# Retention and a multiplicative feed-forward on one core: the third chunk loaded and worked ahead of the weights

## The chip, the core and the metric

The kernel runs on one core of a Trainium2 chip. The metric is the device time of one execution in microseconds (us). The profile is of one execution, and its span runs from the first to the last instruction of the program. TensorE does the matrix products (PE in the profile, its weight loads PEld), VectorE is DVE, ScalarE ACT, GpSimd POOL, and SyncE SP; SP issues all transfers here.

## What is computed

```python
def _attn_ref(q, k, v):                      # (4, 8, 768, 64) each
    gamma = 1.0 - 2.0 ** (-5.0 - np.arange(H))
    for t in range(S):
        state = gamma[None, :, None, None] * state + np.einsum('bhd,bhe->bhde', k[:, :, t], v[:, :, t])
        y[:, :, t] = scale * np.einsum('bhd,bhde->bhe', q[:, :, t], state)

def _moe_ref(x, w1, w2, w3, w_out):          # x: y as (3072, 512)
    a = x @ w1                               # 512 x 1024
    b = x @ w2                               # 512 x 1024
    h = a * b @ w3                           # 1024 x 1024
    return h @ w_out                         # 1024 x 512
```

A recurrent retention over 768 steps for 4 batches and 8 heads gives x, 3072 tokens of 512 numbers. A feed-forward with a product of two branches follows. All inputs and the output are float32.

## The kernel before

The retention is done in chunks of 128 tokens, 24 in all (`NSTEP`, numbered n), six to a batch. Within a chunk, `scores(n)` (L353) multiplies keys by queries on TensorE, and VectorE masks the result (L364). `kv(n)` (L372) makes keys times values, adds the state carried so far (L390, VectorE) and decays it (L391, GpSimd, "t"). `outputs(n)` (L394) adds the two parts of y and scales them into a tile `XT` of two chunks (L407, VectorE). The inputs of a chunk are loaded by `load_chunk` (L67): q for two chunks at each even n (512 KB in pieces of 512 bytes), k and v for each (256 KB each in pieces of 256 bytes). `casts(n)` (L264) turns them into float16 on GpSimd: q at L270, k at L276, v times a decay at L280 ("vp"). Queries and keys are then transposed: in chunks 0 to 7 on TensorE (`q_transposes`, L288, `transposes`, L337), from chunk 8 on by transfers (`dma_transposes`, L317; "kT" and "qTd"). ScalarE copies the keys into a padded tile KP (L350 and L194 in the early chunks, L342 and L343 later), which the scores wait for.

w3 and w_out depend on no token, so their product is made once at the start (L215 to L258) and replaces both; the chunk's feed-forward is then (x w1)*(x w2) times that product. All weights come as float32 rows of 512 KB into twelve staging tiles (`wst`) and are cast to float16 by ScalarE (L194) or VectorE (L192) with `cast_to`.

The feed-forward goes by blocks of tokens (`bounds`, L517): 256, then 128 and 128, then 256 each. `a_unit` (L434) multiplies by w1 and has ScalarE copy the result to a tile `pa`; `b_unit` (L439) multiplies by w2, and VectorE takes the product of both into HT (L443); `o_unit` (L448) multiplies by the combined weights, and ScalarE scales into `osb`, which SP writes out. A unit is a short run of products: 0.43 us for a or b and 1.73 us for o in the kernel's own list of costs.

The order of the work is written out by hand until chunk 3 (L558 to L682). Each engine takes its instructions in the order written here, and SP issues its transfers in that order too. Block 0 is made row by row of the weights (`by_rows`, L617), so that each row can be used as soon as it is there: four PSUM banks (`four_banks`, L612) hold the eight products with w1, which are copied to two staging tiles (`hold`), and then those with w2. From chunk 4 on, `step(n)` (L519) puts units from a queue (`Queue`, L487) between the parts of the retention: 25% of its share after the scores, 25% after kv, the rest after the outputs. Units become available when their tokens are done.

PSUM has eight banks: one for the tag psT (transposes of keys), psA0, psA1, psK and psY with one each, and three in rotation for psF. In the four-bank products before the change, psF gives three and psY one.

The order of the loads is: four column blocks of w3 alternating with w_out, four rows of w3, chunks 0 and 1, four rows of w1, four of w2, chunks 2 to 5 (L115 to L125); chunks 6 and 7 are issued at L666 and L671.

Of the kernel before, what the change touches and what calls it, by code (L numbers as in the profile page):

```python
# [9 lines left out]
FP = mybir.dt.float32  # L10
HP = mybir.dt.float16
# [7 lines left out]
def kernel(  # L19
# [11 lines left out]
    nc = tc.nc  # L31
# [7 lines left out]
    NP = H // 2  # L39
# [27 lines left out]
    def load_chunk(n):  # L67
        if n >= NSTEP:
            return
        b, c = divmod(n, NCH)  # L70
        tiles = []
        if c % 2 == 0:

            t = ld.tile([128, 2 * 512], FP, tag="q64", name="q64", bufs=3)
            dma_in(
                t[:, :].rearrange("p (h x) -> p h x", x=2 * D),
                q[b, :, c * C : (c + 2) * C, :].rearrange("h (p t) d -> p h (t d)", t=2),
            )
            q_in[n // 2] = t
        for nm, src in (("k", k), ("v", v)):  # L80
            t = ld.tile([128, 512], FP, tag=nm + "32", name=nm + "32")
            dma_in(
                t[:, :].rearrange("p (h d) -> p h d", d=D),
                src[b, :, c * C : (c + 1) * C, :].rearrange("h i d -> i h d"),
            )
            tiles.append(t)
        chunk_in[n] = tiles

    def new_stage():
        return wstage.tile([128, 1024], FP, tag="wst", name="stg")  # L90
# [26 lines left out]
        w3c_st.append(load_w3_columns(i))  # L117
        wo_st.append(load_wo(i))
    w3_st = {f: load_rows(moe_w3, f) for f in range(4, 8)}
    load_chunk(0)  # L120
    load_chunk(1)
    w1_st = [load_rows(moe_w1, d) for d in range(4)]
    w2_st = [load_rows(moe_w2, d) for d in range(4)]
    for n in range(2, 6):
        load_chunk(n)  # L125


# [120 lines left out]
    def w3_mm(f, between=None):  # L248
        t = w3t.pop(f)
        ps = ps_f.tile([128, DM], FP, tag="psF", name="psW")  # L250
        for g in range(8):
            if g == 4 and between:
                between()
            nc.tensor.matmul(  # L254
                ps[:, :], lhsT=t[:, g * 128 : (g + 1) * 128], rhs=WO[g // 2][:, g % 2, :],
                start=(g == 0), stop=(g == 7),
            )
        cast_to(W3O[f][:, :], ps[:, :], False)  # L258
# [3 lines left out]
    Tst = [None]  # L262

    def casts(n):  # L264
        if n >= NSTEP:
            return
        k32, v32 = chunk_in.pop(n)
        if n % 2 == 0:
            q16 = att.tile([128, 1024], HP, tag="q16", name="q16")
            nc.gpsimd.tensor_copy(  # L270
                q16[:, :].rearrange("i (t h d) -> i h t d", t=2, d=D),
                q_in.pop(n // 2)[:, :].rearrange("i (h t d) -> i h t d", t=2, d=D),
            )
            q16s[n // 2] = q16
        k16 = att.tile([128, 512], HP, tag="k16", name="k16", bufs=3)
        nc.gpsimd.tensor_copy(k16[:, :], k32[:, :])  # L276
        vp = VP[n % 3]

        for r in range(2):
            nc.gpsimd.tensor_tensor(  # L280
                vp[:, :, r, r * 64 : r * 64 + 64],
                v32[:, :].rearrange("j (p s e) -> j p s e", s=2, e=64)[:, :, r, :],
                VS[:, :].rearrange("j (p s) -> j p s", s=2)[:, :, r].unsqueeze(2).broadcast_to((128, NP, 64)),
                MULT,
            )
        k16s[n] = k16

    def q_transposes(m, later=False):  # L288

        if m >= DT0 // 2:  # L290
            return
        q16 = q16s.pop(m)
        if m == 0:
            ps = ps_at.tile([128, NP, 2, 128], HP, tag="psA0", name="psTq")
        elif m == 1:
            ps = ps_at.tile([128, NP, 2, 128], HP, tag="psK", name="psTq")
        else:
            ps = ps_f.tile([128, NP, 2, 128], HP, tag="psF", name="psTq")
        for p in range(NP):
            for t in range(2):  # L300
                c0 = t * 512 + p * 128
                nc.tensor.transpose(ps[:, p, t, :], q16[:, c0 : c0 + 128], ident16[:, :])  # L302

        def back(c, on_dve=True):
            qT = att.tile([128, NP, 128], HP, tag="qT", name="qT", bufs=4)
            cast_to(
                qT[:, :, :].rearrange("p a (t i) -> p (a t) i", t=2),
                ps[:, :, :, c * 64 : (c + 1) * 64].rearrange("p a t i -> p (a t) i"), on_dve,
            )
            qTs[2 * m + c] = qT  # L310

        if later:
            return back
        back(0)
        back(1)
# [37 lines left out]
    def scores(n):  # L353
        kp = KP[n % 2]
        am = att.tile([128, NP, 2, 128], HP, tag="am", name="am")
        for half in range(2):
            ps = ps_at.tile([128, 2, 2, 128], FP, tag=f"psA{half}", name=f"psA{half}")
            for i in range(2):
                p = half * 2 + i
                for r in range(2):  # L360
                    nc.tensor.matmul(  # L361
                        ps[:, i, r, :], lhsT=kp[:, p, r, :], rhs=queries(n, p), start=True, stop=True
                    )
            nc.vector.tensor_tensor(  # L364
                am[:, half * 2 : half * 2 + 2, :, :].rearrange("j p s i -> j (p s) i"),
                ps[:, :, :, :].rearrange("j p s i -> j (p s) i"),
                keep[:, :].unsqueeze(1).broadcast_to((128, 4, 128)),
                MULT,
            )
        ATs[n] = am  # L370
# [44 lines left out]
    class Ffn:  # L415
# [17 lines left out]

        def a_unit(self, f):  # L434
            ps = self.mm(W1, f)
            self.pa[f] = fsb.tile([128, TB], FP, tag="pa", name="pa")
            nc.scalar.copy(self.pa[f][:, :], ps[:, :])  # L437

        def b_unit(self, f):  # L439
# [102 lines left out]
    def cast_w(W, st, d, on_dve):  # L542
        cast_to(W[d][:, :], st[d][:, :], on_dve)
# [38 lines left out]
    cast_w3(7, w3_st[7])  # L582
    casts(0)
    casts(1)
    w3_mm(5)
    w3_transpose(7)
    q_transposes(0)
# [4 lines left out]
    w3_mm(7, lambda: transposes(1))  # L592
    outputs(0)
    Tst[0] = t_new
    cast_w(W1, w1_st, 0, False)
    scores(1)
    outputs(1)
    Tst[0] = kv(1)
    cast_w(W1, w1_st, 1, False)
    cast_w(W1, w1_st, 2, False)  # L600
    cast_w(W1, w1_st, 3, True)
    cast_w(W2, w2_st, 0, True)
    cast_w(W2, w2_st, 1, True)


    ffn = [Ffn(a, b - a) for a, b in zip(bounds, bounds[1:])]
    NT = len(ffn)
    f0 = ffn[0]
    hold = [new_stage() for _ in range(2)]
    f0.HT = fsb.tile([128, 8, TB], HP, tag="ht", name="ht", bufs=3)  # L610

    def four_banks():  # L612
        got = [ps_f.tile([128, 2, TB], FP, tag="psF", name="psF") for _ in range(3)]
        last = ps_at.tile([128, NP, 128], FP, tag="psY", name="psYf")
        return [t[:, :, :] for t in got] + [last[:, :, :].rearrange("p (a b) c -> p a (b c)", a=2)]

    def by_rows(W, ps, d):  # L617
        for f in range(8):
            nc.tensor.matmul(  # L619
                ps[f // 2][:, f % 2, :], lhsT=W[d][:, f * 128 : (f + 1) * 128],  # L620
                rhs=XT[0][:, d, :], start=(d == 0 and f % 2 == 0),
                stop=(d == 3 and f % 2 == 1),
            )

    ps = four_banks()
    for d in range(4):
        by_rows(W1, ps, d)
    pa = [hold[i // 2][:, i % 2 * 512 : i % 2 * 512 + 512].rearrange("p (a n) -> p a n", a=2) for i in range(4)]
    for i in range(4):
        cast_to(pa[i], ps[i], i % 2 == 1)  # L630
    cast_w(W2, w2_st, 2, True)
    cast_w(W2, w2_st, 3, False)
    casts(2)
    ps = four_banks()
    for d in range(4):
        by_rows(W2, ps, d)
    for i in range(4):
        nc.vector.tensor_tensor(f0.HT[:, 2 * i : 2 * i + 2, :], pa[i], ps[i], MULT)  # L638
    q_back = []

    def chunk2_inputs():
        q_back.append(q_transposes(1, True))
        q_back[0](0)
        transposes(2)
        q_back[0](1, False)

    def chunk2_scores():
        scores(2)

    f0.o_unit(0, chunk2_inputs)  # L650
    f0.o_unit(1, chunk2_scores)
    casts(3)
    transposes(3)

    for t in range(1, NT):
        late = ffn[t - 1].o_units() if t > 1 else []
        units = ffn[t].ab_units()
        for i in range(0, len(units), 8):
            fill.units += units[i : i + 8] + late[:1]
            late = late[1:]  # L660
        fill.units += late
# [2 lines left out]


    load_chunk(6)  # L666
    t_new = kv(2)
    casts(4)
    outputs(2)
    Tst[0] = t_new  # L670
    load_chunk(7)  # L671
    scores(3)
    fill.run(2)
    t_new = kv(3)
    fill.run(2)
    casts(5)
    outputs(3)
    Tst[0] = t_new
    transposes(4)
    fill.run(1)  # L680
    q_transposes(2)
    fill.run(1)  # L682

    for n in range(4, NSTEP):
        if n != DT0 - 2:
# [33 lines left out]
```

## Time and profile before

| | us |
|---|---|
| median of 4 runs | 196.56 |
| lowest and highest | 196.12, 197.86 |
| the profiled execution: its time | 197.86 |
| the profiled execution: its span | 196.0 |
| its TensorE busy time | 185.2 |
| its VectorE, ScalarE, GpSimd busy time | 114.4, 97.2, 79.9 |

The profile's page shows busy time by engine, and in forty slices of 4.9 us each how full every engine was, in tenths. The chain of waits goes back from the last instruction to whatever released each one. Groups of instructions give the count, the busy time, the mean duration in ns and the idle time ahead of them, with what ended it. The busy time of TensorE includes time in which products overlap in its pipeline, so the pace is better read from start to start. A transfer's time to landing counts from its issue on SP, and includes all that it waits behind.

### The profile page before, as it was taken

To read this page: it belongs to the slowest core of one execution; us is meant where nothing else is said; L and a number is where in the kernel's file an instruction comes from. 1 tells how busy PE (TensorE), PEld (TensorE's weight loads), DVE (VectorE), ACT (ScalarE), POOL (GpSimd) and SP (SyncE) were. 2 spreads that over 40 slices of the span, in tenths; PEclk is the share of its full clock that TensorE was granted. 3 is DMA by queue.
4 is the path that set the end of the run, shared out by engine and by line. 5 is a ranking of instruction groups with operands and counts; after the bars stand their busy time and mean duration, and the time that the engine had idled before them with its cause. 6 is when DMAs were issued, how large, how long until landed. Compare 5 with 4: busy or idle time off the path is not lost.

```text
span 196.0 us, 4673 instructions
## 1 busy us (share of the span) xinstructions
PE 185.2 (95%) x1781; PEld 140.2 (72%) x1781; DVE 114.4 (58%) x215; ACT 97.2 (50%) x189; POOL 79.9 (41%) x137
## 2 busy tenths in 40 slices
PE   6589996999999999999999999999999999999993
PEld 2234565856998879679777887788778877887752
DVE  3224476955877767467565866585557655854220
ACT  6278648407454553546355644464455445533322
POOL 7300260347976756574523444844235442200000
PEclk9999999999999999999999999999999999999999
DMA  6999999979999999999999989979999731111003
GB/s 207 360 389 388 206 306 408 349 152 245 229 255 213 236 197 234 233 183 258 183 222 239 193 184 204 241 194 179 200 243 203 149 99 31 59 54 54 39 32 146
DMA packets 87590, 40.15 MB, mean 205 GB/s; under 512 B 67984, under 2 KB 82576, under 8 KB 87568
## 3 DMA queue, kind: packets, MB, share of 16 engines
q1 hardware_dynamic: 87568, 39.86, 90.0%
q8 instruction: 14, 0.23, 0.5%
q14 instruction: 8, 0.07, 0.1%
HBM read 29.36 MB, written 6.29 MB: 182 GB/s over the span
## 4 chain that ended last, share of the span: by engine, by line
PE 78%; DMA 10%; SPq 3%; DVE 3%; ACT 2%; issue 1%; POOL 0%; ACTq 0%; POOLq 0%; DVEq 0%
PE psF L427 35%; PE psO L453 19%; DMA stg<-in_moe_w_dram 5%; PE psA L361 5%; PE psW L254 4%; DMA v<-in_v_dram 3%; PE psF L619 2%; PE psY L399 2%; PE psY L400 2%; SPq L62 2%; PE psY L402 2%; DMA kT<-k 2%; PE psK L382 2%; SPq L326 1%; PE psTq L302 1%
## 5 line engine op out<-in xcount | busy, mean ns | idle before, releaser
L427 PE MATMUL psF<-xt,w 128*128 128x256 f16 (+1 forms) x768 | 87.1, 264 | 0.0
L427 PEld LDWEIGHTS <-w 128*128 128x128 f16 x768 | 68.0, 98 | 6.8
L443 DVE TENSOR_TENSOR ht<-pa,psF 128x256 f16<-128x256 f32 x88 | 36.7, 417 | 24.9 <-PE psF L427 10.6
L437 ACT COPY pa<-psF 128x256 f32<-128x256 f32 x88 | 32.7, 372 | 35.6 <-PE psF L427 35.1
L364 DVE TENSOR_TENSOR am<-psA,keep 128x512 f16<-128x512 f32 x48 | 30.9, 685 | 22.4 <-PE psA L361 22.4
L453 PE MATMUL psO<-w3o,ht 128*128 128x512 f16 x184 | 43.6, 379 | 0.2 <-DVE ht L638 0.2
L391 POOL TENSOR_TENSOR t<-s,GS 128x512 f16<-128x512 f32 x16 | 20.7, 1294 | 44.4 <-DVE s L390 37.7
L280 POOL TENSOR_TENSOR vp<-v,VS 128x256 f16<-128x256 f32 x48 | 28.6, 616 | 11.5 <-PE psY L402 5.3
L453 PEld LDWEIGHTS <-ht 128*128 128x128 f16 x184 | 17.7, 98 | 17.4 <-DVE ht L638 1.0
L458 ACT ACTIVATE osb<-psO 128x512 f32<-128x512 f32 x23 | 13.7, 597 | 31.5 <-PE psO L453 31.5
L270 POOL CAST q<-q 128x1024 f16<-128x1024 f32 x12 | 12.4, 1036 | 24.2 <-DMA q<-in_q_dram 24.2
L407 DVE TENSOR_TENSOR xt<-psY,YS 128x512 f16<-128x512 f32 x24 | 17.7, 736 | 4.6 <-PE psY L402 3.4
L276 POOL CAST k<-k 128x512 f16<-128x512 f32 x24 | 14.7, 613 | 8.6 <-PE psK L382 7.0
L399 PE MATMUL psY<-am,vp 128*128 128x128 f16 x96 | 16.7, 219 | 1.0 <-DVE am L364 0.9
L361 PEld LDWEIGHTS <-kp 128*128 128x128 f16 x192 | 12.5, 98 | 6.0 <-ACT kp L194 0.7
L400 PE MATMUL psY<-am,vp 128*128 128x128 f16 x96 | 16.7, 219 | 0.0
L212 DVE COPY w3t<-psW 128x1024 f16<-128x1024 f16 x8 | 5.5, 691 | 12.7 <-PE psW L220 9.5
L390 DVE TENSOR_TENSOR s<-psK,t 128x512 f32<-128x512 f32 x16 | 11.0, 689 | 3.1 <-PE psK L382 2.8
L342 ACT COPY kp<-kT 64x512 f16<-64x512 f16 x16 | 9.9, 618 | 4.1 <-DMA kT<-k 3.9
L194 ACT CAST w3h<-stg 128x1024 f16<-128x1024 f32 x8 | 8.3, 1043 | 5.0 <-DMA stg<-in_moe_w_dram 5.0
L400 PEld LDWEIGHTS <-vp 128*128 128x128 f16 x96 | 9.4, 98 | 1.5 <-issue 1.2
L361 PE MATMUL psA<-qTd,kp 128*128 128x128 f16 x128 | 9.9, 219 | 0.3 <-ACT kp L343 0.3
(69 smaller groups left out, 174.5 us busy)
## 6 DMA issues: line engine op xcount, KB each, us to landing
stg<-in_moe_w_dram SPq DMA_DIRECT2D x16, 512.0 KB, 8.7
q<-in_q_dram SPq DMA_DIRECT2D x12, 512.0 KB, 5.3
k<-in_k_dram SPq DMA_DIRECT2D x24, 256.0 KB, 5.4
v<-in_v_dram SPq DMA_DIRECT2D x24, 256.0 KB, 5.7
out_dram<-osb SPq DMA_DIRECT2D x23, 256.0 KB, 2.6
stg<-in_moe_w_out_dram SPq DMA_DIRECT2D x4, 512.0 KB, 8.9
kT<-k SPq DMA_TRANSPOSE x16, 4.3
out_dram<-osb SPq DMA_DIRECT2D x2, 128.0 KB, 1.7
```

Source lines behind the costliest of these rows:

```text
L276: nc.gpsimd.tensor_copy(k16[:, :], k32[:, :])
L280: nc.gpsimd.tensor_tensor(vp[:, :, r, r * 64 : r * 64 + 64], v32[:, :].rearrange("j (p s e) -> j p s e", s=2, e=64)[:, :, r, :], VS[:, :]. ...
L361: nc.tensor.matmul(ps[:, i, r, :], lhsT=kp[:, p, r, :], rhs=queries(n, p), start=True, stop=True)
L364: nc.vector.tensor_tensor(am[:, half * 2 : half * 2 + 2, :, :].rearrange("j p s i -> j (p s) i"), ps[:, :, :, :].rearrange("j p s i -> j ( ...
L391: nc.gpsimd.tensor_tensor(t16[:, :, :], s32[:, :, :], GS[:, :, :], MULT)
L399: nc.tensor.matmul(ps[:, p, :], lhsT=vp[:, p, 0, :], rhs=am[:, p, 0, :], start=True, stop=False)
L400: nc.tensor.matmul(ps[:, p, :], lhsT=vp[:, p, 1, :], rhs=am[:, p, 1, :], start=False, stop=(c == 0))
L407: nc.vector.tensor_tensor(XT[n // 2][:, :, n % 2 * C : (n % 2 + 1) * C].rearrange("p a (i t) -> p a t i", t=2), ps[:, :, :].rearrange(orde ...
L427: nc.tensor.matmul(ps[:, i * w : (i + 1) * w], lhsT=W[d][:, (f + i) * 128 : (f + i + 1) * 128], rhs=XT[self.tok0 // TB][:, d, c0 : c0 + w] ...
L437: nc.scalar.copy(self.pa[f][:, :], ps[:, :])
L443: nc.vector.tensor_tensor(self.HT[:, f : f + TB // self.width, :].rearrange("p f n -> p (f n)"), self.pa.pop(f)[:, :], ps[:, :], MULT,)
L453: nc.tensor.matmul(psO[:, :], lhsT=self.HT[:, f, tb * 128 : (tb + 1) * 128], rhs=W3O[f][:, :], start=(f == 0), stop=(f == 7),)
```

## The change

Chunk 2 is loaded ahead of w1 and w2, and is cast (`casts(2)`) right after chunk 1. Its query and key transposes, its scores, its `kv(2)` and its `outputs(2)` move ahead of or between the products of block 0 with w1. One row of w1 is cast on GpSimd instead of ScalarE. The w1 products of block 1 (chunk 2, 128 tokens: four a-units of two 128-column blocks each) are made between the w1 and the w2 products of block 0, and are held in a third staging tile. The bank psT takes the place of psY in the four-bank products. The last two rows of w2 are taken bank by bank, not row by row. The four b-units of block 1 follow, with chunk 3's key transposes between them. The o-units of block 0 are put at the head of the queue. Loads of chunk 7 and the casts and transposes of chunks 4 and 5 change places with other work.

```diff
-    load_chunk(0)
-    load_chunk(1)
+    for n in range(3):
+        load_chunk(n)
     w1_st = [load_rows(moe_w1, d) for d in range(4)]
     w2_st = [load_rows(moe_w2, d) for d in range(4)]
-    for n in range(2, 6):
+    for n in range(3, 6):
         load_chunk(n)
...
         def a_unit(self, f):
             ps = self.mm(W1, f)
-            self.pa[f] = fsb.tile([128, TB], FP, tag="pa", name="pa")
+            if f not in self.pa:
+                self.pa[f] = fsb.tile([128, TB], FP, tag="pa", name="pa")
             nc.scalar.copy(self.pa[f][:, :], ps[:, :])
...
     casts(1)
+    casts(2)
     w3_mm(5)
...
     outputs(0)
     Tst[0] = t_new
-    cast_w(W1, w1_st, 0, False)
     scores(1)
+    q_back = q_transposes(1, True)
+    q_back(0)
+    transposes(2)
     outputs(1)
+    q_back(1, False)
+    nc.gpsimd.tensor_copy(W1[0][:, :], w1_st[0][:, :])
     Tst[0] = kv(1)
     cast_w(W1, w1_st, 1, False)
+    scores(2)
     cast_w(W1, w1_st, 2, False)
-    cast_w(W1, w1_st, 3, True)
-    cast_w(W2, w2_st, 0, True)
-    cast_w(W2, w2_st, 1, True)
...
-    hold = [new_stage() for _ in range(2)]
+    hold = [new_stage() for _ in range(3)]
...
-        last = ps_at.tile([128, NP, 128], FP, tag="psY", name="psYf")
-        return [t[:, :, :] for t in got] + [last[:, :, :].rearrange("p (a b) c -> p a (b c)", a=2)]
-
-    def by_rows(W, ps, d):
-        for f in range(8):
+        got = [ps_t.tile([128, 2, TB], FP, tag="psT", name="psTf")] + got
+        return [t[:, :, :] for t in got]
+
+    def by_rows(W, ps, d, fs=range(8)):
+        for f in fs:
...
-    for d in range(4):
-        by_rows(W1, ps, d)
+    by_rows(W1, ps, 0)
+    t_new = kv(2)
+    by_rows(W1, ps, 1)
+    by_rows(W1, ps, 2)
+    cast_w(W1, w1_st, 3, True)
+    outputs(2)
+    Tst[0] = t_new
+    by_rows(W1, ps, 3)
...
-        cast_to(pa[i], ps[i], i % 2 == 1)
+        cast_to(pa[i], ps[i], i % 2 == 0)
+    cast_w(W2, w2_st, 0, True)
+
+    for f in range(0, 8, 2):
+        ffn[1].pa[f] = hold[2][:, f * 128 : f * 128 + 256]
+        ffn[1].a_unit(f)
+    cast_w(W2, w2_st, 1, True)
     cast_w(W2, w2_st, 2, True)
     cast_w(W2, w2_st, 3, False)
-    casts(2)
+    casts(3)
     ps = four_banks()
-    for d in range(4):
-        by_rows(W2, ps, d)
+    by_rows(W2, ps, 0)
+    by_rows(W2, ps, 1)
+    for i in range(4):
+        for d in range(2, 4):
+            by_rows(W2, ps, d, (2 * i, 2 * i + 1))
     for i in range(4):
         nc.vector.tensor_tensor(f0.HT[:, 2 * i : 2 * i + 2, :], pa[i], ps[i], MULT)
...
-    f0.o_unit(0, chunk2_inputs)
-    f0.o_unit(1, chunk2_scores)
-    casts(3)
+    ffn[1].b_unit(0)
+    ffn[1].b_unit(2)
     transposes(3)
-
-    for t in range(1, NT):
-        late = ffn[t - 1].o_units() if t > 1 else []
+    ffn[1].b_unit(4)
+    ffn[1].b_unit(6)
+
+    fill.units = f0.o_units()
+    for t in range(2, NT):
+        late = ffn[t - 1].o_units()
...
     load_chunk(6)
-    t_new = kv(2)
+    load_chunk(7)
+    fill.run(1)
+    scores(3)
     casts(4)
-    outputs(2)
-    Tst[0] = t_new
-    load_chunk(7)
-    scores(3)
-    fill.run(2)
     t_new = kv(3)
-    fill.run(2)
-    casts(5)
+    fill.run(1)
     outputs(3)
     Tst[0] = t_new
+    casts(5)
+    q_transposes(2)
     transposes(4)
-    fill.run(1)
-    q_transposes(2)
-    fill.run(1)
+    fill.run(2)
```

More of the change, by code (lines that the diff above doesn't have):

```diff
@@ L294, in q_transposes @@
             ps = ps_at.tile([128, NP, 2, 128], HP, tag="psA0", name="psTq")
-        elif m == 1:
-            ps = ps_at.tile([128, NP, 2, 128], HP, tag="psK", name="psTq")
         else:
@@ L625 @@
     ps = four_banks()
-    for d in range(4):
-        by_rows(W1, ps, d)
+    by_rows(W1, ps, 0)
[6 more added lines that the diff above has]
+    by_rows(W1, ps, 3)
     pa = [hold[i // 2][:, i % 2 * 512 : i % 2 * 512 + 512].rearrange("p (a n) -> p a n", a=2) for i in range(4)]
     for i in range(4):
-        cast_to(pa[i], ps[i], i % 2 == 1)
+        cast_to(pa[i], ps[i], i % 2 == 0)
[4 more added lines that the diff above has]
+    cast_w(W2, w2_st, 1, True)
     cast_w(W2, w2_st, 2, True)
     cast_w(W2, w2_st, 3, False)
-    casts(2)
+    casts(3)
     ps = four_banks()
-    for d in range(4):
-        by_rows(W2, ps, d)
+    by_rows(W2, ps, 0)
[3 more added lines that the diff above has]
+            by_rows(W2, ps, d, (2 * i, 2 * i + 1))
     for i in range(4):
         nc.vector.tensor_tensor(f0.HT[:, 2 * i : 2 * i + 2, :], pa[i], ps[i], MULT)
[L639 to L648, printed above, removed]
-    f0.o_unit(0, chunk2_inputs)
-    f0.o_unit(1, chunk2_scores)
-    casts(3)
-    transposes(3)
-    for t in range(1, NT):
-        late = ffn[t - 1].o_units() if t > 1 else []
+    ffn[1].b_unit(0)
+    ffn[1].b_unit(2)
+    transposes(3)
+    ffn[1].b_unit(4)
[3 more added lines that the diff above has]
+        late = ffn[t - 1].o_units()
         units = ffn[t].ab_units()
```

## The prediction, as made before the result was known

> **What bounds the kernel now.** I read the page's busy rows first, then the table of stretches, TensorE's waits, the chain of waits and, around its odd places, the timeline and the transfers' times to landing. The table of stretches gives, for each stretch, its length and the busy time of each engine; the last three numbers are the granted clock, the share of DMA time and GB/s.
>
> ```profile
> PE 185.2 (95%) x1781; PEld 140.2 (72%) x1781; DVE 114.4 (58%) x215; ACT 97.2 (50%) x189; POOL 79.9 (41%) x137
> PE   6589996999999999999999999999999999999993
> DMA  6999999979999999999999989979999731111003
> ```
> ```profile
> 24.00:37.40 13.40, 11.82 (x119) 8.73 (x118) 10.02 (x16) 6.91 (x11) 5.25 (x8) 1.00 1.02 360
> 37.40:41.30 3.90, 3.84 (x32) 3.02 (x31) 2.00 (x4) 1.54 (x3) 0.00 (x0) 1.00 1.03 207
> 41.30:53.30 12.00, 11.34 (x141) 8.43 (x141) 8.81 (x17) 5.87 (x12) 9.90 (x14) 1.00 1.02 222
> 53.30:81.40 28.10, 27.85 (x333) 23.53 (x332) 19.60 (x39) 13.01 (x29) 19.13 (x27) 1.00 1.20 225
> 81.40:196.00 114.60, 111.32 (x1043) 87.72 (x1043) 64.98 (x126) 54.85 (x119) 39.52 (x52) 1.00 0.80 157
> ```
> TensorE is the bound from about 24 us on, at full clock. The DMA engines are just as full until 81 us (shares of 1.02 to 1.20), and only after that do they have room. So there are two bounds in the stretch that the change rewrites. A moved product can gain only TensorE's idle time, and only if no transfer sets a later date that TensorE must keep anyway.
>
> TensorE's named waits after 30 us are few:
>
> ```profile
> PE psY L399 <- DVE am L364: 0.9, 1, 0.9
> PE psF L619 <- DVE xt L407: 0.6, 1, 0.6
> PE psA L361 <- ACT kp L194: 0.4, 1, 0.4
> PE psO L453 <- DVE ht L638: 0.2, 1, 0.2
> ```
> Taking each matmul at the pace of the chain (0.055 us for 128 moving columns, 0.109 for 256, 0.217 for 512) and counting from start to start, TensorE idles some 2.4 us in 24 to 37.4 us and 2.4 us in 37.4 to 53.3 us, of which 1.8 us lie between the end of the w2 products (41.2) and chunk 4's scores (53.33). That is the purse. The chain of waits names the second bound:
>
> ```profile
> 70.59 5.98 DMA v<-in_v_dram
> 76.58 3.62 DMA kT<-k
> 80.19 0.02 issue
> ...
> 80.86 0.62 ACT kp L343
> 81.48 0.05 issue
> 81.53 0.56 PE psA L361 x7
> ```
> The scores of chunk 9 wait for the transposed keys kT, which land at 80.2 us, and then for ScalarE's copies. TensorE idles 0.51 us there. Why is kT late? Its k16 was cast at 67.70 to 68.31, but its issue on SP comes at 76.58, behind the loads of chunks 10 and 11 and an output. From 20 to 98 us SP's issues follow each other within 0.1 us but for a few: SP is held back by the transfers in front, not by TensorE. GpSimd shows the same: its casts start as data lands.
>
> ```profile
> 63.97 1.04 POOL L270 CAST q<-q 128x1024 f16<-128x1024 f32 x1 [0.54 <-DMA q<-in_q_dram]
> ```
>
> **The change, part by part.**
>
> *Chunk 2 ahead of the weights.* Issue plus time to landing gives the dates: last v of chunk 1 22.65+4.6 = 27.2 us; first w1 row 23.69+5.5 = 29.2; last w2 row 28.26+10.0 = 38.3; chunk 2's q 29.17+12.3 = 41.5, k 42.5, v 43.65. The weight rows land about 1.3 us apart. Moved in front, chunk 2's three transfers push all eight rows. Cost from above: as they ran before, 43.65-38.27 = 5.4 us. From below: the first q took 1.8 us after its predecessor (21.16 to 22.95), each k and v 1.0 to 1.1: 3.9. I take 1.9+1.1+1.1 = 4.1 us, since chunk 2 would again follow k and v pieces as in the stretch from 23 us. Here a rule: the Trainium skill (DMA: Bandwidth & Descriptors, Specifications) puts the least piece for full rate at 512 bytes. q's rows are 512-byte pieces, so by the rule q costs what a weight row of equal size does, 1.3 us, and the shift is 3.5; the rows of this trace (1.8 to 3.2 us for q) speak for 4.1. So the w1 rows land at about 33.2, 34.5, 35.8, 37.1, those of w2 at 38.4 to 42.3. Chunk 3 then ends where it did (45.8), as the same bytes are ahead of it.
>
> *Chunk 2's preparation and scores* (0.45 transposes of q, 0.22 of k, 0.45 scores), kv(2) 0.22 and outputs(2) 0.66: 2.00 us of TensorE, moved, not removed. They now stand before and between the w1 products. q lands at 29.1, GpSimd casts it (1.04) by 30.2 and k (0.62) by 30.9. So TensorE, which ends chunk 1's scores at 30.7, has both transposes done by 31.4. outputs(1), behind them, waited until 31.82 for the masked scores already: no cost. scores(2) run at 33.0.
>
> *The w1 row on GpSimd.* No row shows that cast; the nearest is q's cast of the same 128x1024 elements, 1.04 us. Landing 33.2, ready 34.3, against a first w1 product at 33.73 now. ScalarE and VectorE lose that cast; behind it on GpSimd queue t(1) (L391, 1.27 us), wanted by outputs(2) only at 37.8, and casts(3), whose data land later. Against it speaks the Trainium skill (SBUF — State Buffer, "Who interferes with whom"): a VectorE cast between SBUF tensors can take the port pair shared with GpSimd, and the second to issue is blocked to the end. The row agrees in kind: t took 1.65 us at 34.33, beside w casts on VectorE, against a median of 1.27. But at 33.2 to 34.3 VectorE has s(1) and the masks of scores(2), which read PSUM; by the rule's worst case one cast (0.68) is added, by the row 0.38, by the order of work nothing. I take nothing.
>
> *The w1 rows then set TensorE's pace*: d0 34.35 to 35.2, kv(2), d1 from 35.6 (ScalarE's 1.05 after landing), d2 36.9 to 37.8, outputs(2) to 38.4, d3 to 39.3 (was 37.3). ScalarE and VectorE empty the four banks; the staging tile's four a-products (8x0.055 = 0.44 each, 1.76) take the freed banks from 40.0 and, waiting for copies of 0.6 to 0.7 us, end at 42.05. The w2 rows 0 to 2 are cast on VectorE by 42.8 (each 0.68), row 3 on ScalarE at 42.45 to 43.5; products 42.05 to 45.55. Thus the staged products cover the late w2 entirely. The end of the w2 products moves from 41.2 to 45.55, 4.35 later, with 2.00+1.76 = 3.76 of later work done: 0.6 us lost.
>
> *After that* the old order had 10.34 us of products in 41.2 to 53.33, 1.79 idle. The new: four b-products and chunk 3's transposes 1.98, two o-products 3.46, scores, kv and outputs of chunk 3 1.33, chunk 4's transposes 0.67, two products of the next block 0.88: 8.32, and some 0.35 waiting for banks: 54.2. But chunk 4's key transposes now stand later, with 0.88 us of products behind them, while ScalarE's two copies take 1.2: scores(4) at 54.6. Four units (1.76 us) more are done by then, so the old order's equal is 55.09: 0.5 us ahead. Steps 4 and 5 have less filler left (six units and one o-product instead of ten and one), so scores(5) again wait, about 0.4 us, for the same copies. Into step 6 TensorE is 0.1 us ahead (ends: 0.9 ahead if these copies stay covered; 1.9 behind if chunk 2 takes 5.4 us and the cast is blocked 0.68). From step 6 the program is the same.
>
> *Loads of chunk 7* move ahead of the two first outputs on SP; those outputs' buffers aren't wanted soon, and the sum in front of chunk 8 is unchanged: nothing, hidden by the full transfer queue.
>
> **Sum.** 0.1 us of lead, which meets kT of chunk 9. All transfers before it are the same bytes in a queue that never runs dry, so it lands at 80.2 again and scores(9) start at 81.5. A lead is waited away there; a lag of up to 0.5 us vanishes there too. Change of the end: 0. The profiled execution has a span of 196.0 and a time of 197.86, the four runs a median of 196.56; I put the change on the median: 196.56+0, rounded to **196.5 us**.
>
> **Rivals.** *A, slower: the w1 rows come later than TensorE can fill.* All w1 and w2 products stand in order behind the first GpSimd cast. With 0.1 of lead and 0.5 of waiting at chunk 9, each us that this cast is ready after 34.9 us costs one at the end. Chunk 2 at its old 5.4 us makes it 1.3 late and the block 0.68 more: 34.3+1.98 = 36.3, end 1.4 later, 197.9; a further us of dips in the transfers (they ran nearly dry from 40.4 to 42) gives 199. For it: q's 3.2 us. Against: the stretch from 23 us.
>
> *B, faster: the transfer queue gains as well.* That dip of about 1.5 us comes as the w2 rows give way to q; with chunk 3's k and v behind w2 it may shrink, kT of chunk 9 lands at 79, and a lead of 0.5 to 0.9 plus the 0.51 is kept: 195.1 to 195.6. Against: the first weights gave way to q without such a loss.
>
> *C, the change does all it could*: all idle from 37.4 to 53.3 (2.4) and 0.5 at chunk 9 go: 193.7. Against: bank waits and ScalarE's copies that I count in the new order, and the landing of kT.
>
> *D, the moved work is hidden anyway* and the time the same is my forecast.
>
> **From cases to numbers.** D 0.62, A 0.22, B 0.09, C 0.07. Likeliest: 196.5, own range 195.8 to 197.2. The range of 8 in 10 takes in B and A's first mechanism: 195.1 to 198.2. A measurement of this kernel can tell about 1% (2 us) from no change: faster by more, below 194.6, is C and a sliver of B, 0.08; slower by more, above 198.5, is A's upper half with the blocked cast, 0.14; the rest 0.78.
>
> **What would show it.** Right: first w1 product near 34.3, w2 products ending near 45.5, scores(4) near 54.6, kT of chunk 9 landing at 80.2 with a TensorE wait of 0.5 to 0.6 us before its scores. Wrong: first w1 row landing after 34 (A); kT of chunk 9 landing before 79.5 (B); TensorE waiting for W2 rows; a GpSimd cast of W1 above 1.1 us.

## The result, and the profile after

The changed kernel takes 197.45 us in the median of 43 runs (196.92 to 198.13), the kernel before 196.52 in 64 (195.83 to 197.96). The ratio is 1.0043, with a 95% interval of 1.0034 to 1.0053: slower by 0.85 us (0.67 to 1.04). The forecast was no change, 196.5. The time lies in the range, but the change is clear of the noise.

The traced execution after took 197.42 us with a span of 195.6, so its span is *shorter* than that of the traced execution before (196.0). That is the first thing to understand: the traced execution after sits at its kernel's median, the one before 1.3 us above its own. Time less span is 1.7 to 1.9 us in every run of these two kernels, so the difference lies inside the span.

The page after, the same rows as before:

```profile
PE 185.5 (95%) x1781; PEld 140.4 (72%) x1781; DVE 114.4 (58%) x215; ACT 96.9 (50%) x188; POOL 80.3 (41%) x138
PE   6598998989999999999999999999999999999993
DMA  5999999999999999999989999979899731111103
```
The work is the same, and it moved: TensorE's seventh slice (29.4 to 34.3 us) went from 6 to 8 tenths, but the ninth (39.2 to 44.1) from 9 to 8. The table of stretches after (length, busy time of each engine, then granted clock, DMA share and GB/s), cut at the end of the w2 products and at chunk 4's scores:

```profile
24.00:37.40 13.40, 12.40 (x139) 9.23 (x136) 10.20 (x17) 7.32 (x11) 9.53 (x13) 1.00 1.06 324
37.40:45.40 8.00, 7.01 (x80) 5.98 (x78) 5.19 (x9) 3.61 (x7) 1.12 (x2) 1.00 0.99 280
45.40:54.50 9.10, 8.88 (x107) 6.56 (x104) 6.07 (x13) 3.31 (x6) 6.11 (x10) 1.00 1.22 233
```
In the middle row TensorE is busy for 7.0 of 8.0 us. Its waits after 30 us (engine, line, waited for: us in total, times, longest):

```profile
PE psTf L621 <- ACT w L194: 1.0, 2, 0.8
PE psTf L621 <- POOL w L601: 0.6, 1, 0.6
PE psA L359 <- ACT kp L194: 0.3, 1, 0.3
PE psF L425 <- ACT stg L194: 0.2, 1, 0.2
PE psF L425 <- DVE xt L405: 0.2, 1, 0.2
```
The first two lines name the cast of a weight row, which none of before's lines did. The second is not new as lost time: ahead of the first w1 product TensorE stands for 0.7 us after and stood for 0.76 before, where the line named L407 instead. The chain of waits in 38 to 60 us (start, length, what) begins with the longest of them:

```profile
31.52 11.20 DMA stg<-in_moe_w_dram
42.72 0.02 issue
42.74 1.05 ACT w L194
43.80 0.05 issue
43.84 0.41 PE psTf L621 x2
```
The last w2 row lands at 42.72, ScalarE casts it, and TensorE goes on at 43.84, having stood since 42.93 (the last two products begun at 42.71, and 0.109 each): 0.9 us. What comes after that row is therefore dated by it.

Why so late? From issue and time to landing, w1's last row came at 29.62+6.7 = 36.3 and w2's first at 30.09+8.7 = 38.8: 2.5 us apart, where all other w1 and w2 rows of that trace are 1.27 to 1.38 apart. The transfers of 36.0 to 36.8 us by queue show one piece that is no data (packets, MB, share):

```profile
q1 hardware_dynamic: 87, 0.31, 96.7%
q8 instruction: 1, 0.02, 8.5%
```
The piece is an instruction fetch of 16 KB, starting at 36.28. It took 1.09 us of one of the 16 DMA engines (8.5% of 16 engines for 0.8 us). A weight row arrives in sixteen parts, and the trace has the time of each. Of w2's first row fifteen parts are there at 37.55, 1.35 after the same part of w1's last row, and the sixteenth comes at 38.76. The last w2 row is the same: fifteen parts by 41.48, the sixteenth at 42.72. So from the fetch on one part of sixteen comes 1.2 us behind the others, and every row waits for it.

### The profile page after: what moved, and what is told of

The parts are those of the page before. It is cut to its first block, busy times and chain, and to the rows that moved or that the text cites. A ratio compares the mean times of both kernels' runs of the same rounds, so it can differ in the third digit from the quotient of the medians.

```text
span 195.6 us, 4665 instructions
## 1 busy us (share of the span) xinstructions
PE 185.5 (95%) x1781; PEld 140.4 (72%) x1781; DVE 114.4 (58%) x215; ACT 96.9 (50%) x188; POOL 80.3 (41%) x138
## 4 chain that ended last, share of the span: by engine, by line
PE 79%; DMA 12%; SPq 3%; ACT 2%; DVE 2%; issue 1%; ACTq 0%; DVEq 0%
PE psF L425 37%; PE psO L452 20%; DMA stg<-in_moe_w_dram 12%; PE psA L359 5%; PE psW L254 4%; SPq L62 3%; PE psY L397 2%; PE psY L398 2%; PE psY L400 2%; PE psK L380 2%; PE psTq L300 1%; PE psO L469 1%; PE psT L346 1%; PE psW L229 1%; ACT kp L194 1%
## 5 line engine op out<-in xcount | busy, mean ns | idle before, releaser
L442 DVE TENSOR_TENSOR ht<-pa,psF 128x256 f16<-128x256 f32 x84 | 35.0, 417 | 22.9 <-ACT pa L436 10.7
L436 ACT COPY pa<-psF 128x256 f32<-128x256 f32 x84 | 31.3, 373 | 32.8 <-PE psF L425 32.4
L457 ACT ACTIVATE osb<-psO 128x512 f32<-128x512 f32 x23 | 13.7, 598 | 34.3 <-PE psO L452 34.3
L400 PE MATMUL psY<-qTd,t 128*128 128x128 f16 x56 | 10.1, 219 | 0.0
```

Source lines behind the costliest of these rows:

```text
L442: nc.vector.tensor_tensor(self.HT[:, f : f + TB // self.width, :].rearrange("p f n -> p (f n)"), self.pa.pop(f)[:, :], ps[:, :], MULT,)
```

## Experiments

The theory was that two waits make the loss: the last w2 row, and copies that the thinner filler of chunks 3 to 5 no longer covers (0.32 for chunk 3's scaled output at 53.58, 0.22 and 0.49 for padded keys within the scores of chunks 4 and 5, from start to start). In after's timeline these are the steps into the second, within the third and into the last row (128 columns take 0.055 us each):

```profile
53.04 0.39 PE L346 MATMUL psT<-ident,k 128*128 128x128 f16 x4
53.58 1.07 PE L425 MATMUL psF<-xt,w 128*128 128x128 f16 x16 [0.15 <-DVE xt L405]
54.48 0.84 PE L359 MATMUL psA<-qT,kp 128*128 128x128 f16 x8
58.51 0.22 PE L359 MATMUL psA<-qT,kp 128*128 128x128 f16 x1
59.05 0.56 PE L359 MATMUL psA<-qT,kp 128*128 128x128 f16 x7 [0.33 <-ACT kp L194]
```
The rivals: GpSimd's cast of the w1 row; a date set by transfers at chunk 9, as forecast; and something peculiar in the traced execution before.

| kernel | median us | ratio to before, 95% interval |
|---|---|---|
| before, again | 196.90 | 1.0022 (0.9997 to 1.0047) |
| before, loads of chunk 2 ahead only | 200.43 | 1.0185 (1.0138 to 1.0231) |
| before, chunk 9's keys first | 196.71 | 1.0007 (0.9990 to 1.0024) |
| before, chunk 3's keys early and chunk 9's first | 196.49 | 0.9979 (0.9963 to 0.9996) |
| before, chunk 3's keys early only | 196.77 | 1.0003 (0.9970 to 1.0035) |
| before, last w2 row not loaded | 196.07 | 0.9969 (0.9947 to 0.9990) |
| after | 197.45 | 1.0043 (1.0034 to 1.0053) |
| after, w1 row on ScalarE | 197.37 | 1.0045 (1.0026 to 1.0064) |
| after, no staged products | 199.65 | 1.0138 (1.0100 to 1.0175) |
| after, o-product behind chunk 4's transposes | 196.86 | 1.0006 (0.9985 to 1.0027) |
| the same, w3 product in the gaps | 196.77 | 1.0023 (1.0006 to 1.0041) |
| the same, and chunk 9's keys first | 196.95 | 1.0020 (1.0004 to 1.0036) |
| after, last w2 row not loaded | 196.55 | 0.9991 (0.9976 to 1.0007) |
| after, o-product behind, last w2 row not loaded | 196.13 | 0.9957 (0.9939 to 0.9974) |

The kernels ran in four groups beside runs of before, whose medians were 196.49, 196.54, 196.84 and 196.91 (196.52 beside after), so differences are read from the ratios here, at 196.5 us to 1. The three kernels without the last w2 row leave out a load and so compute something else; they serve as measurements alone.

**Two more traces of before.** No edit.

> The kernel before, unchanged, for a second trace of it. The traced execution before took 197.86, 1.3 above the median of 196.52, while the traced execution after (197.42) is at its median: so the two spans (196.0 and 195.6) do not stand for the two medians. Theory (the trace before was a slow draw): a new trace has a time near 196.5 and a span near 194.7, and the 1.3 us are found ahead of or at the scores of chunk 9, most likely as an earlier first transfer and no wait for chunk 9's keys. Rival (the difference lies outside the span): the span is again near 196.0 with a time near 196.5. The ratio to the kernel before is 1.000 within 0.001.

> A third trace of the kernel before. If its time is near the median of 196.5, the wait ahead of chunk 9's scores should be under 0.3 us (theory: the typical execution has little of it); if the wait is 0.5 or more at that time, the theory falls and the difference lies at the first transfers alone.

The first took 197.24 with a span of 195.4, the second 197.06 with 195.3: neither drew a median execution. The ratio of the first came out at 1.0022 where 1.000 within 0.001 was expected, its interval including 1: a difference of 0.2% between two rows of the table is not told from none. But all traces can be cut at marks: where the last w3 row and the v of chunk 1 land, and the start of chunk 8's scores. Chunk 1's v is the last load ahead of what the change moves.

| trace | its time | last w3 row landed | chunk 1's v landed | from the w3 row to chunk 8's scores | from v to chunk 8's scores | from there to the end |
|---|---|---|---|---|---|---|
| before | 197.86 | 21.16 | 27.23 | 53.24 | 47.17 | 121.55 |
| before, again | 197.24 | 20.41 | 26.91 | 53.34 | 46.84 | 121.64 |
| before, third | 197.06 | 20.64 | 26.75 | 53.03 | 46.91 | 121.67 |
| before, chunk 9's keys first | 195.96 | 19.44 | 26.82 | 53.60 | 46.22 | 121.02 |
| after | 197.42 | 20.60 | 26.89 | 53.93 | 47.64 | 121.02 |
| after, o-product behind | 196.82 | 20.44 | 27.01 | 53.51 | 46.93 | 121.02 |

The last column is 121.02 wherever TensorE waits for nothing there. The three traces of before have 0.5 to 0.65 more: at chunk 9 in two, and in the third 0.15 at chunk 9 and 0.46 at chunk 10. The w3 row varies by 1.7 us in these traces, v by 0.5: in the fourth the w3 row is early and the loads behind it are not, so the first column is no measure of the start there. Over all sixteen traces v lands at 26.7 to 28.0, in the middle at 26.9. A draw of before that waits for nothing would take 26.9+47.0+121.02, and 1.8 around the span: 196.7, near its median of 196.5; with the 0.6 of waiting it would be 197.3. The same sum for after gives 197.4, its median being 197.45. So the theory's threshold (under 0.3 at chunk 9 near the median) was not tested by a median draw, but the sum points to it; the next run bears on it.

**Chunk 9's keys first**, on before.

```diff
-        if n == DT0 - 2:
+        if n in (DT0 - 2, DT0 - 1):
             load_chunk(n + 4)
...
-        if n != DT0 - 2:
+        if n not in (DT0 - 2, DT0 - 1):
             load_chunk(n + 4)
```


> Before, with the transposing transfer of chunk 9's keys issued on SP ahead of the loads of chunk 11, as step 6 already does for chunk 8 and 10. Both traces of before show TensorE waiting 0.5 to 0.6 us for it. If that wait is in the typical execution of before too, the median falls by 0.4 to 0.6 (196.0); if the typical execution doesn't have it and only the slower draws do, the median falls by less than 0.2 and the upper part of the spread shrinks. Then my sum, made on the traced execution, gave before a wait that it mostly doesn't have.

The keys land at 75.9 instead of 79.1 to 80.2, and chunk 9 waits for nothing. The median doesn't fall (1.0007); the middle half of the runs spans 196.23 to 197.00, that of before in the same group 196.15 to 196.87. The forecast of this run, 0.4 to 0.6 less if the typical execution has the wait, did not come. So the wait that I built on is not worth its 0.5 us to the typical execution. Whether that is because it isn't there, or because the loads let past give it back, this run alone can't say.

**Only the loads.** On before, the first two hunks of the change.

> Before, with chunk 2's loads moved ahead of w1 and w2 and nothing else changed. If late weights are paid in full where no work is put in their place, the w1 products start some 4 us later and the end comes 2.5 to 4 us later (TensorE's work behind is unchanged and has about 1 to 1.5 us of waits that can absorb). If the transfers and not TensorE set the dates at chunk 9, up to 1 us less: 1.5 to 3. If chunk 2's place in the queue costs nothing: within 0.3.

Slower by 3.6 us (1.85% of 196.5; 2.7 to 4.5 in the interval of four runs): the first bracket. Weights that come later are paid nearly in full where no work takes their place. Its chunk 8 scores stand at 57.69 after the last w3 row, 4.5 more than before.

**No staged products.**

```diff
-    for f in range(0, 8, 2):
-        ffn[1].pa[f] = hold[2][:, f * 128 : f * 128 + 256]
-        ffn[1].a_unit(f)
...
+    for f in range(0, 8, 2):
+        ffn[1].pa[f] = hold[2][:, f * 128 : f * 128 + 256]
+    ffn[1].a_unit(0)
     ffn[1].b_unit(0)
+    ffn[1].a_unit(2)
     ffn[1].b_unit(2)
     transposes(3)
+    ffn[1].a_unit(4)
     ffn[1].b_unit(4)
+    ffn[1].a_unit(6)
     ffn[1].b_unit(6)
```


> After, with the four w1 products of chunk 2 not made ahead of w2 but each beside its w2 product; all else as after. My theory is that the last w2 row is what TensorE waits for in after (0.9 us, although 1.76 us of staged products are ahead of it). Then without them the wait grows by about 1.8 less what block evacuation hides (0.3 to 0.8), and the time is 1.0 to 1.5 above after, near 198.6. Rival: a later date (chunk 9's keys, a copy) sets the end, and the time stays within 0.3 of after.

1.9 us above after by the ratios (2.2 by the medians), more than expected. TensorE's waits in 38.5 to 45 us of this trace, as the timeline gives them at the end of a row:

```profile
40.31 0.39 PE L621 MATMUL psTf<-xt,w 128*128 128x256 f16 x2 [1.72 <-DVE w L192]
43.60 0.39 PE L621 MATMUL psTf<-xt,w 128*128 128x256 f16 x2 [1.15 <-ACT w L194]
```
Both w2 casts are now waited for. The staged products do what they are for; they are only not enough.

**The w1 row on ScalarE.**

```diff
-    nc.gpsimd.tensor_copy(W1[0][:, :], w1_st[0][:, :])
+    cast_w(W1, w1_st, 0, False)
```


> After, with the one w1 row cast on ScalarE again, all else as after. Theory (the loss is the late last w2 row and the thin filler): the cast takes 1.05 on either engine, and on ScalarE it delays the casts of rows 1 and 2 by up to 0.3 each, since rows land 1.28 apart and ScalarE takes 1.05: within 0.4 of after (197.2 to 197.8). Rival (GpSimd's cast, or the decay queued behind it, is what made after slower): 0.5 to 1 less than after.

1.0045 against 1.0043: within 0.2%, the GpSimd cast neither costs nor gains. The first rival, 0.5 to 1 us, is out.

**The o-product behind chunk 4's transposes.**

```diff
     ffn[1].b_unit(4)
-    ffn[1].b_unit(6)
...
     t_new = kv(3)
-    fill.run(1)
+    ffn[1].b_unit(6)
     outputs(3)
...
     transposes(4)
-    fill.run(2)
+    fill.run(1)
```


> After, with block 0's second o-product (1.7 us) put behind chunk 4's transposes in place of two short products of the next block, and the last b-product of block 1 between kv and outputs of chunk 3. It tells what the thin filler costs: in after TensorE waits 0.32 for chunk 3's scaled output, 0.22 and 0.49 for key copies ahead of the scores of chunks 4 and 5. If these waits are the loss, 0.7 to 1.0 us less than after (196.5 to 196.8), about the time of before. If transfers set the date of chunk 9, no gain: within 0.2 of after (197.3 to 197.6).

0.7 us below after by the ratios (0.6 by the medians): what was expected, and before is within the interval. The three waits in chunks 3 to 5 are gone from its trace (one of 0.27 came, within chunk 3's outputs, and 0.1 is left in chunk 5's scores), and the last w2 row remains:

```profile
PE psTf L621 <- ACT w L194: 1.2, 2, 1.0
PE psTf L621 <- POOL w L601: 0.6, 1, 0.6
PE psF L425 <- ACT stg L194: 0.2, 1, 0.2
```

**The w3 product in the gaps**, on the kernel just told, and the same with chunk 9's keys first.

```diff
-    w3_mm(7, lambda: transposes(1))
+    transposes(1)
...
     by_rows(W1, ps, 3)
+    w3last = w3t.pop(7)
+    ps7 = ps_at.tile([128, DM], FP, tag="psY", name="psW7")
+
+    def w3_part(gs):
+        for g in gs:
+            nc.tensor.matmul(
+                ps7[:, :], lhsT=w3last[:, g * 128 : (g + 1) * 128], rhs=WO[g // 2][:, g % 2, :],
+                start=(g == 0), stop=(g == 7),
+            )
...
     for f in range(0, 8, 2):
+        if f == 0:
+            w3_part(range(0, 2))
...
     by_rows(W2, ps, 1)
+    w3_part(range(2, 6))
...
+    w3_part(range(6, 8))
+    cast_to(W3O[7][:, :], ps7[:, :], False)
     ffn[1].b_unit(0)
```


> The kernel of the run with the o-product behind chunk 4's transposes, and in it the last w3 product (eight products, 1.73 us) moved from before chunk 0's outputs into TensorE's three waits of block 0: two products at the first staged product, four ahead of the late w2 rows, two ahead of the b-products. If the late last w2 row is a wait for data that other work can fill, TensorE's lead grows by 0.9 to 1.3 us: 195.6 to 196.1, under before. If chunk 9's keys then set the date, 0.3 to 0.5 of it stay: 196.4. If the products taken away at 28 us were covering something there, no gain: 196.9.

> The w3 product in the gaps and the earlier key transpose of chunk 9 together. If the keys of chunk 9 hold back the kernel with the filled gaps, this one is 0.4 to 0.8 below it (195.3 to 195.6); if not, within 0.2 of it.

No gain from either: 1.0023 and 1.0020. My expectation was ill reasoned. The gaps at the w2 rows are filled in the trace, but the product came from *ahead* of them, and it left as much idle time where it was taken (waits for q's and k's casts, then for the first w1 row, which lands when it lands). TensorE's idle time after 24 us is 9.1 us, against 8.9, each with the 3.4 us that follow its last product. Filling these waits could have gained only with work from behind them. As the first brought no lead, the second says nothing about chunk 9.

**The last w2 row not loaded**, on after and on before.

```diff
-    w2_st = [load_rows(moe_w2, d) for d in range(4)]
+    w2_st = [load_rows(moe_w2, d) for d in range(3)]
+    w2_st.append(w2_st[2])
```


> After, without the load of the last row of w2 (row 2's staging tile is cast twice, so the product with w2 is another one); all instructions else stay. It ends the weights about 1.3 us earlier. Theory (the last w2 row is what block 0 of after waits for): the wait of 0.9 to 1.1 ahead of the last w2 products goes, less 0.2 to 0.4 for the copies of the banks that it hid: 0.5 to 0.9 below after (196.5 to 196.9). Rival (the thin filler or later dates set the end): within 0.2 of after.

> Before, without the load of the last row of w2 in the same way. Its last w2 row waits 0 to 0.4 us in three traces (0, 0.27, 0.40). Theory: 0 to 0.4 below before (196.1 to 196.5). If before too hung on its transfers, as my forecast had it, 0.5 to 1 below.

After falls by 1.0 us by the ratios (0.9 by the medians), to 0.9991 of before, and in its trace the stop of 0.9 us ahead of the last w2 products is gone (256 columns take 0.109 us each):

```profile
41.76 0.82 PE L622 MATMUL psF<-xt,w 128*128 128x256 f16 x6
42.42 0.60 PE L622 MATMUL psTf<-xt,w 128*128 128x256 f16 x4
```
Before falls too, by 0.6 us (0.2 to 1.0), more than its 0 to 0.4 of waiting for that row explains at the middle of the interval. Taking out a transfer of 1.3 us also advances everything behind it in a full queue, so this experiment does not take away the wait alone. Both kernels without that row stand in one group, and there after is still 0.4 us slower (0.9991 against 0.9969). So of after's 1.0 only about 0.4 is what after lost to that row and before did not, and the intervals leave 0.5 either way.

**Both waits away.** The o-product behind chunk 4's transposes, and the last w2 row not loaded.

> After, with the o-product behind chunk 4's transposes and without the load of the last w2 row (row 2's staging tile is cast twice, so the product with w2 is another one). Alone the first took 0.6 off, the second 0.9. If these two waits are separate and are the whole loss, they add up: 1.3 to 1.5 below after (195.9 to 196.2 where before has 196.5). If they share a cause, or a later date sets the end, it stays within 0.3 of the second alone (196.3 to 196.6).

0.9957: 0.86% below after, 1.7 us where 1.3 to 1.5 was expected. By the ratios the two alone gave 0.7 and 1.0, so they add up, and no later date takes the lead back. But 1.7 is twice the loss of 0.85, as leaving out the row helps before too. Like with like is this kernel against before without the row: 0.9957 against 0.9969, the same within the intervals. With both waits gone the two kernels take the same time, which is what the prediction gave for the change.

**Chunk 3's keys early**, on before, with and without chunk 9's keys first.

```diff
     def chunk2_scores():
         scores(2)
+        casts(3)
+        transposes(3)
...
     f0.o_unit(1, chunk2_scores)
-    casts(3)
-    transposes(3)
...
     transposes(4)
-    fill.run(1)
     q_transposes(2)
-    fill.run(1)
+    fill.run(2)
```


> Before with the earlier key transpose of chunk 9, and in it chunk 3's casts and key transposes put ahead of the second half of block 0's second o-product, and chunk 4's query transposes ahead of both short products there. The loads stay. Two waits of all traces of before, 0.20+0.55 ahead of chunk 3's scores and 0.24 ahead of chunk 4's, are then covered by products that come later in the order. If TensorE alone sets the end: 0.6 to 1.0 below before (195.5 to 195.9). If chunk 3's k, landing at about 44.0 to 44.7, comes too late for it or the transfers set a later date: 0 to 0.3 below.

> Before, with chunk 3's key transposes and chunk 4's query transposes earlier as in the kernel run before, but with chunk 9's key transfer left in its old place. In the trace of that run a lead of 0.4 to 0.9 us met a wait of 1.1 for the transposed queries of chunk 10. If the loads that were let past cost as much as they gave, this one is as fast as that or faster: 0.4 to 0.8 below before. If the old place brings back a wait of 0.5 or more at chunk 9 once TensorE leads, 0 to 0.2 below before.

With both edits 0.9979, that is 0.4 us (0.1 to 0.7) below before: the only version here, computing all of it, that beats both kernels, and by less than hoped. Without chunk 9's keys first: no gain that can be told (0.9970 to 1.0035). In the trace of the faster one there is a new wait, for chunk 10's transposed queries (1.1 us in all from start to start):

```profile
86.96 0.89 PE L361 MATMUL psA<-qTd,kp 128*128 128x128 f16 x8 [0.69 <-DMA qTd<-q]
```
Here, then, a date set by transfers does hold TensorE up. The single trace without chunk 9's keys first shows no such wait, and none at chunk 9 either (121.01 us from chunk 8's scores to the end), in a draw in which TensorE came late anyway (last w3 row at 21.20, chunk 1's v at 28.0). What decides between these two kernels stays open.

## Why the prediction was wrong, point by point

**Chunk 2's transfers** were sized well: q 1.9, k 1.2, v 1.15 us, 4.3 against my 4.1. By the rule of the Trainium skill (DMA: Bandwidth & Descriptors, Specifications: full rate from 512 bytes on) q would have taken 1.3; the row was right.

**The w1 rows and GpSimd's cast** went as forecast. Counted from the last w3 row (0.56 us earlier in this draw), the first w1 product came at 33.59-20.60 = 13.0, forecast 34.35-21.16 = 13.2. The cast took 1.04 us, and t behind it 1.27, its undisturbed value. So the blocking that the Trainium skill describes (SBUF — State Buffer, "Who interferes with whom") did not come, as no VectorE cast stood beside them:

```profile
32.49 1.04 POOL L601 CAST w<-stg 128x1024 f16<-128x1024 f32 x1
33.78 1.27 POOL L389 TENSOR_TENSOR t<-s,GS 128x512 f16<-128x512 f32 x1 [0.24 <-DVE s L388]
```

**The step that failed first** is "Thus the staged products cover the late w2 entirely". I had the last w2 row ready at 43.5 and, by the same sum, TensorE there at 44.0 (42.05 and eighteen products of 0.109), a margin of 0.5 us, and took the row's date as certain. Counted from the last w3 row I forecast its landing at 21.1; it came at 22.1, and it was ready at 23.2 instead of 22.3. TensorE was there at 22.3, 0.5 earlier than forecast, and stood for 0.9. So the w2 products ended at 24.8 where I had 24.4: 0.4 of loss against the forecast.

The extra 1.0 is the instruction fetch, as far as these traces can show it. In the traces of after, of the w1 row on ScalarE, of no staged products, of the o-product behind and of the two without the last w2 row, the fetch starts at 36.0 to 36.3 us and the next row lands 2.1 to 2.8 us after its predecessor. In the kernels with the w3 product in the gaps it starts at 37.4 and 38.3, and there the row after that is the late one (2.0 and 2.3). The row and the fetch move together, and in all eight the sixteenth part of the row comes 0.7 to 1.5 us behind the fifteenth, the fetch having taken 1.0 to 1.1; no run moved the fetch alone. In before the same fetch fell at 36.6 to 38.5: on the last w2 row (before, again: TensorE waited 0.27), on chunk 2's q (the execution I read), and in the third trace on no transfer that shows it. Its mark was in the trace of before, as q's 3.2 us; I used that row only as a risk to w1. Not every late row has such a piece: in before, again one w1 row came 2.1 us after the one ahead with no fetch beside it, and that stays open.

**The thin filler** I sized at 0.4+0.4. It was 0.32+0.22+0.49 = 1.03. I missed that the two short products which I counted as cover behind chunk 4's transposes need chunk 3's scaled output themselves. Undoing this gave 0.7.

Together these turn the lead of 0.1 us into a lag of 0.7: from the last w3 row to chunk 8's scores 53.93 instead of 53.03 to 53.34. TensorE's idle time by stretch, from start to start, says the same without a mark of the transfers (before: three traces):

| stretch | before | after |
|---|---|---|
| 24 us to the first w1 product | 2.2 | 1.5 |
| to the end of the w2 products | 0.5 to 0.8 | 2.2 |
| to chunk 4's scores | 1.7 to 1.9 | 0.8 |
| to chunk 8's scores | 0.4 | 1.1 |
| all until there | 4.7 to 5.0 | 5.6 |

The change did gain ahead of w1 and behind w2, as it was meant to; it lost more between, and in chunks 4 to 7.

**The step that failed second** is the base: "a lag of up to 0.5 us vanishes there too". In the traces it does nearly vanish. From the last w3 row to the end after takes 174.95 us and the traces of before 174.70 to 174.98, because these wait 0.5 to 0.65 at chunk 9 or 10 and after waits for nothing there: its keys land at 78.7, not "at 80.2 again" (I had taken the queue never to run dry, against my own note that it nearly did from 40.4 to 42 us). In the medians the lag comes through. I had put the change made on an execution 1.3 us slower than the median straight on the median. That the typical execution of before lacks that wait no trace of before shows. It is inferred: from the sum above, from the median that did not fall with chunk 9's keys first, and from the trace of chunk 3's keys early only, which has the transfers of chunk 9 in their old places and no wait. If so, 0.7 of lag, with the 0.1 to 0.2 that these marks can't settle, is the measured 0.85.

**The rivals.** A had the right mechanism, weights later than TensorE can fill, but at w1 and through chunk 2's size; it was w2, through a piece that I had left out. B came in its first half: chunk 9's keys landed 58.1 us after the last w3 row, against 58.5 to 59.2 in the traces of before, but TensorE had no lead to use it. C did not come. Two of the signs named for a wrong forecast did, TensorE waiting for a w2 row and chunk 9's keys ahead of 79.5.

## What to carry to other kernels

A change sized on one traced execution should first be cut at marks that can be compared from draw to draw, and set against the median; a wait that one execution shows may not be in the median, and must not serve as a cushion. Where data-late work is covered by other work with a margin of a few tenths of a microsecond, look for everything else that uses the same transfer engines at that moment, instruction fetches included. And a wait is gained by filling it with work that stands behind it; work taken from ahead only moved the hole here. Where leaving something out is to show what it cost, leave it out of both kernels.

## What was not expected of the hardware

Instruction fetches appear in the same 16 DMA engines as the data: 14 pieces of 16 KB in one execution, 0.93 to 1.42 us each on one engine in the trace of after. From one piece to the next that trace has 216 to 287 of TensorE's instructions (products and weight loads), 255 in the mean, while the counts of the other engines scatter; that the pieces are TensorE's is inferred from this. In the nine traces with chunk 2 ahead, the piece at 36.0 to 39.1 us went with a weight row that landed 0.7 to 1.5 us late. It is not always so: in the third trace of before the piece at 37.08 made nothing late that shows.
